# Finishing the last group of heads in one piece instead of two halves of queries

## The chip, the core and the metric

The kernel runs on one core of one Trainium2 chip. The core has a matrix engine (TensorE, PE in the profile, with its weight loads as PEld), a vector engine (VectorE, DVE), an activation engine (ScalarE, ACT), GpSimd (POOL) and SyncE (SP), which here issues most of the DMAs. Each engine works through its own instructions in the order in which they were written, and engines wait for each other by semaphores. The metric is the time of one execution on the device in microseconds (us).

## What is computed

One layer for 2048 tokens of width 640, with 32 heads of 20 dimensions. The tokens are normalised, and two branches are made from them. Branch A goes through four segments of 512 tokens one after another:

```python
logits = einsum(qs, ks) * scale + mask        # within the segment, causal
a_dot  = einsum(softmax(logits), vs)
a_mem  = (phi(qs) @ M) / (phi(qs) @ z + 1e-6) # memory of the segments before
o      = g * a_mem + (1.0 - g) * a_dot        # g: one gate per head
M, z   = M + phi(ks)^T @ vs, z + sum(phi(ks))
```

and its result is multiplied by `wo`. Branch B is a gated network on the same normalised tokens: `(sigmoid(x @ w_gate) * (x @ w_up)) @ w_down`, with 1536 hidden columns. The output is `x + A * silu(B)`.

## The kernel before

**The pieces of attention.** The 32 heads are treated as eight groups of four (`NG = 8`). A segment has four blocks of 128 queries and four blocks of 128 keys. A *unit* is one filling of a score tile `Sps` of 128 x 4 x 512 (four heads): `scores` writes it with TensorE (line 542), `exps` takes the exponential on ScalarE into `pt` (line 550) and cuts off the part above the diagonal with one GpSimd instruction for each key block in the unit (line 552). Two groups need five units, because a key block kb only meets the query blocks kb to 3: the last pair of groups (6 and 7 of segment 3) has the units (6: kb 0), (6: kb 1 and kb 3), (6: kb 2 and 7: kb 2), (7: kb 0) and (7: kb 1 and kb 3).

**The product with V.** In nearly all groups the product with V is made transposed (`attend_T`, tile `ApsT`). The last pair of groups takes another way, `attend` (lines 592 to 618): for each head and each query block from kb up, one small matmul (line 606, 128 x 21 out, the 21st column being the sum of the weights) adds into one PSUM tile `Aps` of 128 x 4 query blocks x 4 heads x 21. The parts of `Aps` written by the key block kb are the query blocks kb to 3. Key blocks come in the order in which the units deliver them; for group 7 this is 2, 0, 1, 3. So kb 1 is the third (12 matmuls) and kb 3 the fourth (4 matmuls, on query block 3 alone).

**Finishing a group.** `finalize(n, g, q0, q1)` divides by the sum of weights, applies the gate and adds to `odot`, which already holds the memory's part. It is four VectorE instructions over the query blocks q0 to q1:

```python
nc.vector.reciprocal(rd[:, 0:nq, :], Aps[:, q0:q1, :, DH])            # line 625
nc.vector.tensor_tensor(rd..., rd..., omg[...], op=ALU.mult)          # line 626
nc.vector.tensor_tensor(od..., Aps[:, q0:q1, :, 0:DH], rd..., mult)   # line 630
nc.vector.tensor_tensor(dst, dst, od, op=ALU.add)                     # line 632, dst: odot
```

Group 6 is finished by one such call over all four query blocks. Group 7 is finished by two: query blocks 0 and 1 after the third key block, query blocks 2 and 3 after the fourth.

**What stands around it.** All order is written out by hand: the program's text is a sequence of calls, and the events with times in `TIMES` and the dense work (the matmuls of branch B) are merged when the program is built, by a count of TensorE time (`fill`, `step`). `finalize` has no part in that count. In the last stage the dense work is the product with `w_down` (`do_down`, tile `yp`, 12 matmuls of 128 x 320 for each of 8 pieces; then ScalarE's tanh at line 448 into `t`, and VectorE's product at line 449 into `aa`). The PSUM tiles of all of this come from one pool of four buffers (`ps_d`).

**The tail** (lines 926 to 946). Two pieces of `yp` were held back. The first is made, then `tail_T4(0, 2)` transposes the last 128 columns of `odot` for the query blocks 0 and 1 on TensorE (line 517, tile `po`), ScalarE copies them to `oT` (line 518), and `tail_piece` multiplies by `wo` (line 526, tile `sp`, five matmuls of 128 x 320; the fourth of them takes its operand from `oTm`). `oTm` comes from `tail_sum` (line 512), one VectorE addition behind a transposing DMA of `odot` columns 384 to 511 (line 508), none of which are written by group 7's finishing. After the pieces of rows 0, the second held piece of `yp` and row block 1 comes `tail_T4(2, 4)` for the query blocks 2 and 3. The rest is products (line 528), additions (line 534) and output DMAs (lines 537 and 940).

Of the kernel before, what the change touches and what calls it, by code (L numbers as in the profile page):

```python
# [19 lines left out]
NG = 8  # L20
# [55 lines left out]
def kernel(  # L76
# [513 lines left out]
    acc = dict(group=None, todo=[])  # L590

    def attend(n, unit, pt):

        todo = acc["todo"] + [(p, pt) for p in unit]
        acc["todo"] = []
        for i, ((g, kb, c0, ncol, q0), t) in enumerate(todo):
            if acc["group"] is None:
                acc["group"], acc["blocks"], acc["fresh"] = g, 0, True
                acc["ps"] = ps_d.tile([P, 4, 4, E1], F32, name="Aps", tag="d")
            if acc["group"] != g or (acc["blocks"] == 0 and i > 0 and todo[i - 1][0][0] != g):  # L600
                acc["todo"] = todo[i:]
                break
            for r in range(4):
                for qb in range(kb, 4):
                    off = c0 + (qb - kb) * P
                    nc.tensor.matmul(acc["ps"][:, qb, r, :], lhsT=t[:, r, off:off + P],
                                     rhs=V[n % 2][:, kb, 4 * g + r, :],
                                     start=acc["fresh"], stop=True, skip_group_check=True)
                    acc["fresh"] = False
            acc["blocks"] += 1  # L610
            split = g == NG - 1
            if acc["blocks"] == 3 and split:
                finalize(n, g, 0, 2)
            if acc["blocks"] == 4:
                finalize(n, g, 2 if split else 0, 4)
                acc["group"] = None
                acc["todo"] = todo[i + 1:]
                break

    def finalize(n, g, q0, q1):  # L620

        s, Aps = seg[n], acc["ps"]
        nq = q1 - q0
        rd = opool.tile([P, 4, 4], F32, name="rd", bufs=3)
        nc.vector.reciprocal(rd[:, 0:nq, :], Aps[:, q0:q1, :, DH])
        nc.vector.tensor_tensor(rd[:, 0:nq, :], rd[:, 0:nq, :],
                                omg[:, 4 * g:4 * g + 4].unsqueeze(1).to_broadcast([P, nq, 4]), op=ALU.mult)
        dst = s["odot"][:, q0:q1, 4 * g * DH:(4 * g + 4) * DH]
        od = opool.tile([P, 4, 4 * DH], BF, name="od", tag="tb", bufs=1)[:, 0:nq, :]
        nc.vector.tensor_tensor(od.rearrange("p q (r e) -> p q r e", e=DH), Aps[:, q0:q1, :, 0:DH],  # L630
                                rd[:, 0:nq, :].unsqueeze(3).to_broadcast([P, nq, 4, DH]), op=ALU.mult)
        nc.vector.tensor_tensor(dst, dst, od, op=ALU.add)
# [134 lines left out]
    for p in range(0, OLD, 5):  # L767
        n, g = units[p][0], units[p][1][0][0]
# [16 lines left out]
    def old_attend(slot):  # L785
        attend(NSEG - 1, units[slot][1], pts[slot])
# [111 lines left out]
    for slot, (n, unit) in enumerate(units):  # L898
        if slot in visits:
            m, g, us = visits[slot]  # L900
# [73 lines left out]
```

## Time and profile before

| what | value |
|---|---|
| median of 3 runs | 321.15 us (320.79 to 321.5) |
| the profiled execution: time | 320.71 us |
| the profiled execution: span from first to last instruction | 319.0 us |
| granted TensorE clock, mean | 0.999 |
| PE busy | 311.4 us, 98% of the span |
| DVE, ACT, POOL busy | 229.8, 227.4, 135.4 us |
| DVE instructions | 505 |
| `attend`'s matmuls on `Aps` (line 606) | 80, from 290.1 to 304.3 us |

The page of the profile gives busy times and groups of instructions; the timeline gives each instruction with its start in us from the start of the span, its duration, its engine, its line, `out<-in`, its shape, how many were merged into the row, and in brackets how long the engine had been idle before it and which instruction's end released it. Matmuls overlap in the pipeline: their starts are recorded and their ends are modelled, so one row of merged matmuls runs from the first start to the last modelled end. The chain that ended last is followed back from the last instruction through whatever released each step.

### The profile page before, as it was taken

How to read it: one execution, taken by the hardware profiler on the slowest of the kernel's cores; microseconds unless marked ns; L12 is line 12 of the kernel's file. 1: busy time of each engine (PE TensorE's matmuls, PEld its weight loads, DVE VectorE, ACT ScalarE, POOL GpSimd, SP SyncE). 2: the span in 40 equal slices, each digit the busy share in tenths (PEclk: the TensorE clock that was granted, in tenths of full speed). 3: DMA queues.
4: the chain of work that ended last, by engine and by line, in shares of the span. 5: the costliest groups of instructions: out<-in, count | busy, mean ns of one | idle time of the engine just before them, and what ended most of it. 6: DMA issues, size and time to landing. Idle time of an engine off the chain costs nothing.

```text
span 319.0 us, 10076 instructions
## 1 busy us (share of the span) xinstructions
PE 311.4 (98%) x4244; PEld 167.2 (52%) x4244; DVE 229.8 (72%) x505; ACT 227.4 (71%) x228; POOL 135.4 (42%) x230
## 2 busy tenths in 40 slices
PE   7999999999999999999999999999999999999985
PEld 3644445664545445654675455545566545445653
DVE  6474356656769879997689999977787777635455
ACT  4623577787898877777998678788887766687611
POOL 1870036435263355235453445444443444535312
PEclk9999999999999999999999999999999999999999
DMA  7984986500751462406854534148433001250302
GB/s 253 369 328 134 311 212 173 130 20 4 218 164 56 144 109 105 105 23 199 212 171 123 143 93 126 47 150 202 148 90 116 11 23 43 106 125 2 101 17 82
DMA packets 56085, 41.36 MB, mean 130 GB/s; under 512 B 26952, under 2 KB 54664, under 8 KB 56040
## 3 DMA queue, kind: packets, MB, share of 16 engines
q1 hardware_dynamic: 53496, 35.97, 39.5%
q10 hardware_dynamic: 2544, 4.75, 4.0%
q8 instruction: 33, 0.54, 0.7%
q14 instruction: 12, 0.10, 0.1%
HBM read 19.90 MB, written 14.78 MB: 109 GB/s over the span
## 4 chain that ended last, share of the span: by engine, by line
PE 95%; DMA 2%; ACT 1%; DVE 1%; issue 0%; SPq 0%; ACTq 0%
PE up L124 11%; PE yp L124 11%; PE gp L124 10%; PE psq L124 10%; PE Sps L542 9%; PE gp L128 6%; PE up L128 6%; PE yp L128 6%; PE psv L124 5%; PE ApsT L566 5%; PE psq L128 4%; PE sp L124 3%; PE sp L128 3%; DMA Wv<-in_A_wv_dram 2%; PE sp L526 1%; PE psv L128 1%
## 5 line engine op out<-in xcount | busy, mean ns | idle before, releaser
L550 ACT ACTIVATE pt<-Sps 128x2048 bf16<-128x2048 f32 x80 | 150.2, 1878 | 40.2 <-PE Sps L542 35.4
L552 POOL TENSOR_SCALAR_AFFINE_SELECT pt<-pt 128x512 bf16<-128x512 bf16 x128 | 83.0, 665 | 156.8 <-ACT pt L550 156.7
L432 DVE SCALAR_TENSOR_TENSOR hT<-tg,up 128x512 bf16<-128x512 bf16 x48 | 32.4, 675 | 23.2 <-PE up L124 8.7
L124 PE MATMUL up<-xnT,Wu 128*128 128x512 bf16 x160 | 43.0, 380 | 0.0
L124 PE MATMUL yp<-Wd,hT 128*128 128x320 bf16 x257 | 39.9, 299 | 0.0
L124 PE MATMUL gp<-xnT,Wg 128*128 128x512 bf16 x150 | 39.3, 380 | 0.0
L421 ACT ACTIVATE tg<-gp 128x512 bf16<-128x512 f32 x48 | 28.6, 596 | 14.3 <-PE gp L124 10.9
L542 PE MATMUL Sps<-QT,KT 23*128 23x384 bf16 (+3 forms) x512 | 32.4, 300 | 0.2
L585 DVE STREAM_TRANSPOSE obT<-ob 128x512 bf16<-128x512 bf16 x30 | 21.1, 704 | 13.4 <-POOL ob L581 13.3
L124 PEld LDWEIGHTS <-hT 128*128 128x128 bf16 x257 | 23.5, 98 | 11.7 <-issue 3.2
L449 DVE SCALAR_TENSOR_TENSOR aa<-t,yp 128x320 bf16<-128x320 bf16 x32 | 15.3, 479 | 15.1 <-ACT t L448 14.9
L128 PE MATMUL gp<-xnT,Wg 128*32 128x512 bf16 x360 | 24.1, 380 | 0.0
L587 DVE STREAM_TRANSPOSE tb<-ApsT 128x512 f32<-128x512 f32 x30 | 21.2, 708 | 2.2 <-PE ApsT L566 2.1
L124 PEld LDWEIGHTS <-Wu 128*128 128x128 bf16 x160 | 14.3, 98 | 16.2 <-issue 3.2
L566 PE MATMUL ApsT<-pt,V 128*32 128x512 bf16 (+2 forms) x480 | 22.8, 299 | 0.0
L448 ACT ACTIVATE t<-yp 128x320 bf16<-128x320 f32 x32 | 14.0, 437 | 12.2 <-PE yp L124 10.3
L542 PEld LDWEIGHTS <-KT 23*128 23x128 bf16 x512 | 9.9, 92 | 24.3 <-issue 23.9
L124 PEld LDWEIGHTS <-Wg 128*128 128x128 bf16 x150 | 14.0, 98 | 16.0 <-issue 1.9
L128 PE MATMUL up<-xnT,Wu 128*32 128x512 bf16 x320 | 21.7, 380 | 0.0
L124 PE MATMUL psv<-Wv,xnT 128*128 128x320 bf16 x130 | 20.4, 299 | 0.3 <-ACT xnT L666 0.2
L581 POOL TENSOR_TENSOR ob<-tb,rb 128x320 bf16<-128x320 f32 x27 | 19.8, 733 | 2.3
L128 PE MATMUL yp<-Wd,hT 128*32 128x320 bf16 x508 | 20.0, 300 | 0.0
(122 smaller groups left out, 448.5 us busy)
## 6 DMA issues: line engine op xcount, KB each, us to landing
KT<-Kd SPq DMA_DIRECT2D x32, 80.0 KB
QT<-Qd SPq DMA_DIRECT2D x32, 80.0 KB
out_dram<-xt SPq DMA_DIRECT2D x14, 160.0 KB
Wg<-in_B_w_gate_dram ACTq DMA_DIRECT2D x1, 1920.0 KB
Wu<-in_B_w_up_dram ACTq DMA_DIRECT2D x1, 1920.0 KB
xt<-in_A_x_dram SPq DMA_DIRECT2D x3, 640.0 KB
Wd<-in_B_w_down_dram SPq DMA_DIRECT2D x1, 1920.0 KB
Xd<-xn SPq DMA_DIRECT2D x12, 160.0 KB
```

What stands on the lines that cost most here:

```text
L124: nc.tensor.matmul(out_, lhsT=lhsT, rhs=rhs, start=start, stop=stop, skip_group_check=True)
L128: nc.tensor.matmul(out_[cols], lhsT=lhsT[:, cols], rhs=rhs, start=start, stop=stop, tile_position=(0, 32 * r), skip_group_check=True)
L421: nc.scalar.activation(tg[:], gp[:], ACT.Tanh, scale=0.5)
L432: nc.vector.scalar_tensor_tensor(out=h[:], in0=seg[n]["tg"][:], scalar=1.0, in1=up[:], op0=ALU.add, op1=ALU.mult)
L449: nc.vector.scalar_tensor_tensor(out=s["aa"][j][:, hs], in0=t2[:], scalar=1.0, in1=yp[:], op0=ALU.add, op1=ALU.mult)
L542: nc.tensor.matmul(Sps[:, r, c0:c0 + ncol], lhsT=KT[32 * r:32 * r + DH + 3, g, kb * P:(kb + 1) * P], rhs=QT[32 * r:32 * r + DH + 3, g, q0: ...
L550: nc.scalar.activation(pt[:, :, 0:ntot], Sps[:, :, 0:ntot], ACT.Exp, scale=SCALE)
L552: nc.gpsimd.affine_select(out=pt[:, :, c0:c0 + P], in_=pt[:, :, c0:c0 + P], compare_op=ALU.is_ge, fill=0.0, base=0, pattern=[[0, 4], [1, P ...
L566: nc.tensor.matmul(ps[32 * r:32 * r + 32, q0:L], lhsT=Vflat[n % 2][:, off:off + 32], rhs=t[:, r, c0:c0 + ncol], start=(i == 0), stop=(i == ...
L581: nc.gpsimd.tensor_tensor(ob[:, :, 0:DH], tb[:, :, 0:DH], rb[:].unsqueeze(2).to_broadcast([P, L // 32, DH]), op=ALU.mult)
L585: nc.vector.transpose(s["obT", g // 4][:, g % 4, :], ob[:].rearrange("p b e -> p (b e)"))
L587: s["turn", g] = (lambda: nc.vector.transpose(tb[:].rearrange("p b e -> p (b e)"), ps[:]), quotients, turn_back)
```

## The change

Group 7 is no longer finished in two calls. The call over the query blocks 0 and 1 after its third key block goes, and the call after its fourth key block covers all four query blocks, as for group 6. No other call, tile or DMA is changed.

```diff
             acc["blocks"] += 1
-            split = g == NG - 1
-            if acc["blocks"] == 3 and split:
-                finalize(n, g, 0, 2)
             if acc["blocks"] == 4:
-                finalize(n, g, 2 if split else 0, 4)
+                finalize(n, g, 0, 4)
                 acc["group"] = None
                 acc["todo"] = todo[i + 1:]
                 break
```

## The prediction

> **What bounds the kernel now.** I read the page first, for what bounds the whole, then the timeline of the last 24 us, where group 7 is finished, then the waits and the chain there, and last a table of half microseconds around the spot.
>
> Page, busy times and the chain that ended last:
>
> ```profile
> PE 311.4 (98%) x4244; PEld 167.2 (52%) x4244; DVE 229.8 (72%) x505; ACT 227.4 (71%) x228; POOL 135.4 (42%) x230
> ...
> PE 95%; DMA 2%; ACT 1%; DVE 1%; issue 0%; SPq 0%; ACTq 0%
> ```
>
> TensorE bounds it: a microsecond in which TensorE stands still is one lost, unless it is waited for again later. DVE holds 1% of the chain, so there are places where the chain leaves TensorE. One is the edited place. Timeline of 295 to 319 us:
>
> ```profile
> 298.15 0.25 DVE L625 RECIPROCAL rd<-Aps 128x16 f32<-128x16 f32 x1
> ...
> 298.43 0.17 DVE L626 TENSOR_TENSOR rd<-rd,omg 128x16 f32<-128x16 f32 x1
> ...
> 298.64 0.49 DVE L630 TENSOR_TENSOR od<-Aps,rd 128x320 bf16<-128x320 f32 x1
> 299.17 0.32 DVE L632 TENSOR_TENSOR odot<-odot,od 128x320 bf16<-128x320 bf16 x1
> ...
> 299.38 0.75 PE L606 MATMUL Aps<-V,pt 128*128 128x21 bf16 x24
> ...
> 302.29 0.51 PEld L606 LDWEIGHTS <-pt 128*128 128x128 bf16 x13
> 302.43 0.45 PE L606 MATMUL Aps<-V,pt 128*128 128x21 bf16 x12
> ...
> 302.96 0.49 DVE L449 SCALAR_TENSOR_TENSOR aa<-t,yp 128x320 bf16<-128x320 bf16 x1 [0.56 <-ACT t L448]
> 303.37 0.20 DVE L625 RECIPROCAL rd<-Aps 128x8 f32<-128x8 f32 x1
> 303.61 0.17 DVE L626 TENSOR_TENSOR rd<-rd,omg 128x8 f32<-128x8 f32 x1
> 303.81 0.32 DVE L630 TENSOR_TENSOR od<-Aps,rd 128x160 bf16<-128x160 f32 x1
> 304.16 0.24 DVE L632 TENSOR_TENSOR odot<-odot,od 128x160 bf16<-128x160 bf16 x1
> 304.18 0.25 PE L606 MATMUL Aps<-V,pt 128*128 128x21 bf16 x4 [1.30 <-DVE od L630]
> ...
> 304.28 3.28 PE L124 MATMUL yp<-Wd,hT 128*128 128x320 bf16 x23
> 304.46 0.21 DVE L625 RECIPROCAL rd<-Aps 128x8 f32<-128x8 f32 x1
> ...
> 305.27 0.24 DVE L632 TENSOR_TENSOR odot<-odot,od 128x160 bf16<-128x160 bf16 x1
> ...
> 306.85 0.41 DVE L512 TENSOR_TENSOR oTm<-oTm,oT 96x512 bf16<-96x512 bf16 x1
> 307.27 0.23 PEld L517 LDWEIGHTS <-odot 128*128 128x128 bf16 x2
> ```
>
> The first four rows are group 6 finished in one piece. Then group 7: 12 matmuls of key block 1 at 302.43, and the 4 of key block 3 only at 304.18. They write query block 3, the first half's DVE work reads query blocks 0 and 1, and still they wait until its last read of `Aps` (line 630, to 304.13) is over: idle 1.30 us, released by DVE. The thirteenth weight load in the row at 302.29 is the first of key block 3's, so its `pt`, mask included, was there; only `Aps` was missing. The list of TensorE's waits in this stretch has this one entry alone, and the chain runs through it (ACT 302.49, DVE 302.96 to 304.14, PE 304.18).
>
> Half microseconds (busy of each engine with counts, clock, DMA share, GB/s):
>
> ```profile
> 303.00:303.50 0.50, 0.00 (x0) 0.00 (x0) 0.50 (x2) 0.00 (x0) 0.00 (x0) 1.00 0.92 210
> 303.50:304.00 0.50, 0.00 (x0) 0.00 (x0) 0.43 (x3) 0.00 (x0) 0.00 (x0) 1.00 0.17 33
> 304.00:304.50 0.50, 0.32 (x6) 0.28 (x6) 0.41 (x3) 0.00 (x0) 0.00 (x0) 1.00 0.00 0
> ```
>
> A whole microsecond has no matmul and only DVE at work; the DMA share is the transposing transfer into `oTm`, whose bytes end before 304.
>
> **The change part by part.** Sums are against the profiled execution: 319.0 us of span and 1.71 around it, 320.71, which is 0.44 below the median of the three runs.
>
> *Removed: the wait of key block 3.* Nothing on DVE now stands between the 12 matmuls and the 4. How long is the gap really? The idle column says 1.30, from the modelled end of the twelfth matmul (302.88) to 304.18. But small matmuls follow each other at their starts: the 24 of the row at 299.38 last 0.75 less 0.17 for the last one alone, so 0.58 for 23 steps, 0.025 a step. Listed one by one, the twelfth of key block 1 starts at 302.71; the next would start at 302.735 instead of 304.18: 1.44 us. The row of 24 is also followed by a `yp` matmul at 299.99, before its own end at 300.13. So I take 1.44, from recorded starts, and keep 1.30, the idle column, as the lower end. The Trainium skill (Perfetto Trace Analysis, section Tensor Engine Instruction) says that the profiler estimates the end of a matmul from its size instead of observing it; by that page the idle column understates this gain, and the trace agrees, with 299.99 against 300.13.
>
> *Removed: four DVE instructions.* Two halves cost 2 x (0.20 + 0.17 + 0.32 + 0.24) = 1.86 us busy; one piece costs as group 6's, 0.25 + 0.17 + 0.49 + 0.32 = 1.23. The 0.63 saved is worth nothing by itself: after 305.51 DVE idles 0.94 until its next product.
>
> *Moved: the finishing of query blocks 0 and 1 goes behind the 4 matmuls.* These then end at about 302.98 (302.735, three steps, 0.17). DVE is at line 449 until 303.45 anyway, so the first reciprocal stays at 303.37, and from there group 6's piece takes 299.49 - 298.15 = 1.34: all four blocks are in `odot` at 304.71, where before blocks 0 and 1 were at 304.40 and blocks 2 and 3 at 305.51. No DMA is issued by it, and it passes nothing on the queues of SP, POOL or ACT.
>
> *What is late next.* Everything behind on TensorE comes 1.44 earlier, and each item's supplier must follow:
> - The transposes of `odot` blocks 0 and 1 (weights at 307.27) move to 305.83; `odot` is ready at 304.71: cover 1.12, before 2.87. Without it, each further microsecond would be lost in full.
> - DVE's next product (306.44) moves to 305.00; the piece ends at 304.71: cover 0.29. It is queued behind it on DVE; were it late, it would delay the addition at line 512 first, which has the next cover.
> - Line 512 (306.85 to 307.26) moves to 305.41 to 305.82; its reader, the first matmul on `oTm`, has its weights at 307.79, then 306.35: cover 0.53, as now. Line 512 also needs the transposing DMA. Its bytes end before 304; when its semaphore came, the trace doesn't show, only that it was by 306.85. Bounds: it came with the bytes, 0 lost; or at 306.85, and then line 512 can't move, ends at 307.26, and the 306.35 load waits 0.91. The nearest row is the spill before it (line 504): bytes until shortly after 301, its successor released at 301.63. So some half microsecond, 304.5, and nothing is lost.
> - The PSUM buffer of `Aps` is free after line 630, at about 304.4 (before 305.23), for a tile that TensorE writes from 305.9 on: no wait.
> - ScalarE's copy of `po` keeps TensorE waiting 0.47 at 307.9, and the last DVE additions and stores take 3.7 us after the last matmul. Both hang on the matmuls alone and move with them.
>
> *Sum*: 319.0 - 1.44 = 317.56 of span; 319.27 for a profiled execution; 321.15 - 1.44 = 319.7 for the median, 0.45% less.
>
> **The rivals.**
> 1. *The transfer takes the place of the wait.* If the semaphore of the transposing DMA comes as late as 306.85, the load of `oTm` waits 0.91, and 0.53 of the gain stays: 320.6, 0.16% less. For it: the trace hides the landing. Against: bytes ended some 3 us before that.
> 2. *The change doesn't do what it says.* The 4 matmuls wait as long for something else, such as GpSimd's mask of key block 3 or the tile's former reader: 321.15. Against: the mask's row ends at 302.50 and the weights made from it were loaded before the stall.
> 3. *Slower: the piece, now whole, comes behind other DVE work.* Before, blocks 0 and 1 had 2.87 us until the transposes; now the transposes need the whole piece. If it ended after 305.83, TensorE would wait; from 307.27 the gain is gone, from 307.9 the kernel is slower by over 0.2%. The place would be behind the product at line 449 of the last `yp` before the transposes (308.07, then 306.63): from some 307.04 to 308.38, a wait of 2.55, 1.1 more than is won: 322.3. Against: the two calls stand in one event with nothing between them on DVE, and what stands ahead of the first half now (the product at 302.96) is what stands ahead of the piece then. For it: DVE is 72% busy, and in the rows above its instructions run one behind the other. The Trainium skill (Perfetto Trace Analysis, section Tensor Engine Instruction) states for DVE that its queue is strictly first in, first out, which speaks against joining the halves: a piece behind late work can't pass it. The trace agrees so far: the reciprocal of 303.37 started only as the product of 302.96 ended, though its matmuls had ended by 302.88.
>
> **How the numbers follow.** Forecast 0.83, rival 1 0.07, rival 2 0.05, rival 3 0.05. The three runs of before lie within 0.11% of their median, so a difference of about 0.2%, 0.64 us, is what can be told from none. Faster by more than that: the forecast, 0.83. Within it: rivals 1 and 2, 0.12. Slower: rival 3, 0.05. The forecast's own range is 321.15 less 1.44 or 1.30, with 0.4 of scatter on either side (the runs' half spread of 0.35 and a little for a second median): 319.3 to 320.25. The range goes a little lower, to 319.2, and up to rival 1 with a little scatter, 320.7.
>
> **What would show it.** Right: no wait of line 606 for DVE; 16 matmuls on `Aps` in one row from about 302.4, 0.55 long, and the 23 of `yp` from about 302.84; lines 625 to 632 twice each in the whole trace, all with 16 or 320 elements, and 501 DVE instructions; the piece from 303.4 to 304.7; line 512 near 305.4 and the weights of the transposes near 305.8 with no wait for DVE; a span near 317.6. Wrong: an idle time of TensorE before line 517 released by line 632 (rival 3), before the first matmul on `oTm` released by line 512 with DVE waiting for the DMA (rival 1), or a row of 4 matmuls on `Aps` still by itself (rival 2). The weakest term is the landing of the transfer; the stall itself is seen in one execution only, and a shorter one in the others would shrink the gain.

## The result and the profile after

The changed kernel takes 319.65 us (median of six runs, 319.48 to 320.62) against 321.49 us for the kernel before in the same comparison: ratio 0.9949, 95% interval 0.9932 to 0.9966. By the ratio that is 1.6 us less, between 1.1 and 2.2; the two medians are 1.84 apart. Forecast were 319.7 us and a gain of 1.44.

One number on the page misleads. The profiled execution of the changed kernel has a span of 318.9 us, as long as the 319.0 of before: it is the slowest of the six (320.62). Timeline of TensorE in the first 22 us, first the changed kernel, then the kernel before:

```profile
6.70 1.14 PE L124 MATMUL psv<-Wv,xnT 128*128 128x320 bf16 x5 [0.74 <-DMA Wv<-in_A_wv_dram]
...
11.54 2.88 PE L124 MATMUL psv<-Wv,xnT 128*128 128x320 bf16 x20
```

```profile
6.26 0.85 PE L124 MATMUL psv<-Wv,xnT 128*128 128x320 bf16 x5 [0.24 <-ACT xnT L666]
...
10.52 2.88 PE L124 MATMUL psv<-Wv,xnT 128*128 128x320 bf16 x20
```

The twenty matmuls start 1.02 us later in this execution, in which the first matmuls waited for the load of `Wv`. By the edited place the delay is 1.39 (303.82 against 302.43 for the first matmul of key block 1). Most of the last 0.37 arises at one row of `psv` at 168.5 us, of the same code in both: the delay is 1.12 ahead of it and 1.40 behind, and in the changed kernel TensorE stands idle there for 0.26 without a releaser that the profile shows. None of this lies near the edit. So the two profiles are compared from a mark inside them, the start of that first matmul of group 7's key block 1, to the start of the last addition on line 534. This *tail stretch* ends with these rows, first before, then changed:

```profile
315.99 0.32 DVE L534 TENSOR_TENSOR xt<-aa,xt 128x320 bf16<-128x320 bf16 x1
```

```profile
315.94 0.32 DVE L534 TENSOR_TENSOR xt<-aa,xt 128x320 bf16<-128x320 bf16 x1
```

It is 315.99 - 302.43 = 13.56 us before, and 315.94 - 303.82 = 12.12 us after: 1.44 less. The 13.56 come from one profile; for the other executions of the kernel before there are only the total times.

Timeline of the changed kernel at the edited place (its lines 622 to 629 are the lines 625 to 632 of before):

```profile
303.69 0.59 PEld L606 LDWEIGHTS <-pt 128*128 128x128 bf16 x16
303.82 0.55 PE L606 MATMUL Aps<-V,pt 128*128 128x21 bf16 x16
...
304.23 3.28 PE L124 MATMUL yp<-Wd,hT 128*128 128x320 bf16 x23
304.36 0.49 DVE L449 SCALAR_TENSOR_TENSOR aa<-t,yp 128x320 bf16<-128x320 bf16 x1 [0.56 <-ACT t L448]
304.76 0.25 DVE L622 RECIPROCAL rd<-Aps 128x16 f32<-128x16 f32 x1
305.04 0.18 DVE L623 TENSOR_TENSOR rd<-rd,omg 128x16 f32<-128x16 f32 x1
305.25 0.49 DVE L627 TENSOR_TENSOR od<-Aps,rd 128x320 bf16<-128x320 f32 x1
305.78 0.32 DVE L629 TENSOR_TENSOR odot<-odot,od 128x320 bf16<-128x320 bf16 x1
...
306.79 0.41 DVE L512 TENSOR_TENSOR oTm<-oTm,oT 96x512 bf16<-96x512 bf16 x1
307.21 0.23 PEld L517 LDWEIGHTS <-odot 128*128 128x128 bf16 x2
```

Both key blocks' 16 matmuls are one row with no wait, the 23 of `yp` begin 0.41 us behind its start (before: 304.28 - 302.43 = 1.85), and the piece on DVE ends at 306.10, 1.11 us ahead of the transposes' weights.

### The profile page after: what moved, and what is told of

It is laid out like the page before. It is cut to its first block, busy times and chain, and to the rows that moved or that the text cites. A ratio compares the mean times of both kernels' runs of the same rounds, so it can differ in the third digit from the quotient of the medians.

```text
span 318.9 us, 10072 instructions
## 1 busy us (share of the span) xinstructions
PE 311.6 (98%) x4244; PEld 166.9 (52%) x4244; DVE 229.3 (72%) x501; ACT 227.2 (71%) x228; POOL 135.1 (42%) x230
## 3 DMA queue, kind: packets, MB, share of 16 engines
q10 hardware_dynamic: 2544, 4.75, 4.0%
## 4 chain that ended last, share of the span: by engine, by line
PE 95%; DMA 2%; ACT 1%; DVE 1%; issue 0%; SPq 0%; ACTq 0%
PE up L124 11%; PE yp L124 11%; PE gp L124 10%; PE psq L124 10%; PE Sps L542 9%; PE gp L128 6%; PE up L128 6%; PE yp L128 6%; PE ApsT L566 5%; PE psv L124 5%; PE psq L128 4%; PE sp L124 3%; PE sp L128 3%; DMA xt<-in_A_x_dram 2%; PE sp L526 1%; PE psv L128 1%
```

## The experiments

All are read by the tail stretch, which comes from one profiled execution of each kernel; where a ratio is given, more executions were timed. Theory: the gain is TensorE's wait for the first half's reads of `Aps`, and nothing else.

**The changed kernel again, twice**, beside the other kernels.

> The changed kernel again, as the measure for the others. All expectations speak of the tail stretch: from the start of the first matmul of group 7's key block 1 on Aps to the start of the last addition on line 534 (before 315.99 - 302.43 = 13.56 us, changed kernel 315.94 - 303.82 = 12.12 us). Theory (the gain is TensorE's wait for the first half's reads of Aps, 1.44 us): 12.12 again, ratio about 0.9955. Rival (the opening of the kernel scatters and part of the measured gain is that): ratio nearer to 1, stretch unchanged.

Measured: ratio 0.9952 (0.9934 to 0.9969), stretch 315.05 - 302.93 = 12.12. So the gain is not one lucky comparison: ratio and stretch agree within the interval (1.44 of 321.2 is 0.9955). But this profile shows something that the first did not, at the transfer into `oTm` (SPq is the queue on which SyncE issues DMAs):

```profile
302.08 1.16 SPq L508 DMA_TRANSPOSE oTm<-Od  x1
...
306.57 0.57 PE L526 MATMUL sp<-Wo,oT 128*128 128x320 bf16 x3
...
306.69 0.42 DVE L512 TENSOR_TENSOR oTm<-oTm,oT 96x512 bf16<-96x512 bf16 x1 [0.71 <-DMA oTm<-Od]
...
307.17 0.10 PEld L526 LDWEIGHTS <-oTm 128*128 128x128 bf16 x1 [0.36 <-DVE oTm L512]
307.17 0.31 PE L526 MATMUL sp<-Wo,oTm 128*128 128x320 bf16 x1
...
307.41 0.72 PE L526 MATMUL sp<-Wo,oT 128*128 128x320 bf16 x4
```

Here the addition of line 512 waited for the transposing DMA, until 4.61 us after its issue, and the matmul on `oTm` waited for the addition. That is rival 1 at work, and yet the stretch is the same. The first changed profile shows why:

```profile
307.46 0.57 PE L526 MATMUL sp<-Wo,oT 128*128 128x320 bf16 x3
...
307.87 0.30 PE L526 MATMUL sp<-Wo,oTm 128*128 128x320 bf16 x1
...
308.30 0.72 PE L526 MATMUL sp<-Wo,oT 128*128 128x320 bf16 x4
```

The matmul behind the one on `oTm` starts 0.84 after the row of three in both (308.30 - 307.46 and 307.41 - 306.57), because it waits for ScalarE's copy of `po`. The one on `oTm` may come up to 0.3 later without loss; here it came 0.19 later.

> The changed kernel once more, beside the two above. Theory: stretch 12.12 whether line 512 waits for the DMA or not, since a wait of up to 0.31 there is taken up by the 0.47 us that the next matmul waits for ScalarE's copy; ratio about 0.9952.

Measured: ratio 0.9952 (0.9938 to 0.9966), stretch 315.85 - 303.73 = 12.12, and the wait for the DMA was there again (0.70 on DVE, 4.41 us after the issue).

**Both halves behind the fourth key block.**

```diff
-            if acc["blocks"] == 3 and split:
-                finalize(n, g, 0, 2)
             if acc["blocks"] == 4:
+                if split:
+                    finalize(n, g, 0, 2)
                 finalize(n, g, 2 if split else 0, 4)
```

> The two halves are kept, eight instructions on DVE, but both stand behind the fourth key block's matmuls. Theory (the wait alone): no wait of line 606 for DVE, the second half ends about 0.7 us later than the one piece, the next product and the addition of line 512 are late by some 0.4 us, which their covers hold: stretch 12.12, ratio about 0.9955. Rival (the gain is four DVE instructions fewer, 0.63 us of DVE, one piece instead of two): the gain goes, stretch near 13.5, ratio near 1.

```profile
303.06 0.55 PE L606 MATMUL Aps<-V,pt 128*128 128x21 bf16 x16
...
303.99 0.20 DVE L625 RECIPROCAL rd<-Aps 128x8 f32<-128x8 f32 x1
...
304.94 0.20 DVE L625 RECIPROCAL rd<-Aps 128x8 f32<-128x8 f32 x1
```

Measured: ratio 0.9948 (0.9930 to 0.9966), stretch 315.17 - 303.06 = 12.11. The eight DVE instructions are all there and the whole gain is too. One piece instead of two, and four instructions fewer, are worth nothing here; the place of the first half was everything.

**Two PSUM tiles for group 7, halves where they were.** The edit is shown in part; the rest of it makes `acc["ps"]` a list and keeps the mark of the first write for each tile.

```diff
+                acc["ps"] += [ps_d.tile([P, 4, 4, E1], F32, name="ApsB", tag="d") if g == NG - 1 else acc["ps"][0]]
...
-                    nc.tensor.matmul(acc["ps"][:, qb, r, :], lhsT=t[:, r, off:off + P],
+                    b = qb // 2 if g == NG - 1 else 0
+                    nc.tensor.matmul(acc["ps"][b][:, qb, r, :], lhsT=t[:, r, off:off + P],
...
-        s, Aps = seg[n], acc["ps"]
+        s, Aps = seg[n], acc["ps"][q0 // 2]
```

> The halves and their places are those of the kernel before, but group 7's query blocks 2 and 3 get a PSUM tile of their own. Theory (the wait is for the tile that both share, not for the split or its place): no wait of line 606 for DVE, stretch 12.1, ratio about 0.9955, unless the fifth tile in a pool of four makes some other matmul wait, which would be seen at its own row. Rival (a half finished between the key blocks holds TensorE whatever tile it reads): the 1.3 us idle before 4 matmuls stays, stretch 13.56, ratio 1.

Measured: ratio 0.9950 (0.9932 to 0.9968), stretch 314.78 - 302.67 = 12.11. Timeline:

```profile
302.92 0.30 PE L608 MATMUL ApsB<-V,pt 128*128 128x21 bf16 x6
...
303.44 0.20 DVE L627 RECIPROCAL rd<-Aps 128x8 f32<-128x8 f32 x1
...
304.40 0.20 DVE L627 RECIPROCAL rd<-ApsB 128x8 f32<-128x8 f32 x1
```

Key block 3's four matmuls run straight on (the last six of the row on `ApsB`), although the first half is called ahead of them: TensorE had waited for the tile that the half reads, not for the half. The Trainium skill (PSUM — Partial Sum Buffer, section PSUM bank collisions raise a hardware error) tells kernels to guard PSUM by bank and group of 32 partitions, not by address; the two traces agree, with 1.30 us of idle for other columns of one tile and none for another tile. The kernel's text names no semaphore: the wait that the trace shows was put in when the program was built. Whether it goes by the tile or by the bank that the tile lies in, and what the hardware would do without it, no run here separates.

**The wait made shorter and longer.** First, the first half copies its part of `Aps` into SBUF and works there:

```diff
+        if nq == 2 and q0 == 0:
+            ac = opool.tile([P, 2, 4, E1], F32, name="ac", bufs=1)
+            nc.vector.tensor_copy(ac[:], Aps[:, q0:q1])
+            Aps = ac
```

> The kernel before, but the first half first copies its part of Aps (128 x 168) into SBUF by one DVE instruction and works from there. Theory (TensorE waits for the last read of Aps, no longer): the copy takes about 0.3 us as the read of 128 x 160 did, so the last read ends near 303.7 instead of 304.13 in the time of before, the wait is about 0.43 shorter, stretch 13.56 - 0.43 = 13.1. Rival (TensorE waits until the half is finished in odot): the half is 0.3 longer, stretch 13.9.

Second, its product on line 630 is done four times, with the same result each time:

```diff
-        nc.vector.tensor_tensor(od.rearrange("p q (r e) -> p q r e", e=DH), Aps[:, q0:q1, :, 0:DH],
-                                rd[:, 0:nq, :].unsqueeze(3).to_broadcast([P, nq, 4, DH]), op=ALU.mult)
+        for _ in range(4 if nq == 2 and q0 == 0 else 1):
+            nc.vector.tensor_tensor(od.rearrange("p q (r e) -> p q r e", e=DH), Aps[:, q0:q1, :, 0:DH],
+                                    rd[:, 0:nq, :].unsqueeze(3).to_broadcast([P, nq, 4, DH]), op=ALU.mult)
```

> The kernel before, with the first half's product on line 630, the last read of Aps, done four times instead of once: 3 x 0.35 = 1.05 us more between the key blocks. Theory: the wait grows by all of it, idle 2.35, stretch 13.56 + 1.05 = 14.6. Rival (some of the wait is set by something other than DVE's reads): less than that is added.

Timeline of the first, then of the second:

```profile
304.00 0.33 DVE L626 COPY ac<-Aps 128x168 f32<-128x168 f32 x1
...
304.38 0.25 PE L606 MATMUL Aps<-V,pt 128*128 128x21 bf16 x4 [0.86 <-DVE ac L626]
```

```profile
304.42 1.40 DVE L631 TENSOR_TENSOR od<-Aps,rd 128x160 bf16<-128x160 f32 x4
...
305.87 0.25 PE L606 MATMUL Aps<-V,pt 128*128 128x21 bf16 x4 [2.38 <-DVE od L631]
```

Measured: stretch 316.19 - 303.06 = 13.13 (expected 13.1) and 317.68 - 303.04 = 14.64 (expected 14.6). The wait goes with the last read of `Aps` to within 0.05 us, in both directions, and all of it arrives at the end of the tail stretch (-0.43 and +1.08 against 13.56).

**The piece made longer.** The same loop around the product, in the changed kernel and for the whole of group 7, three times in the first kernel and five times in the second:

```diff
+        for _ in range(3 if g == NG - 1 else 1):
```

> The changed kernel, with group 7's product on line 627 done three times instead of once: the piece is 2 x 0.53 = 1.06 us longer. By the covers as the prediction had them (0.29 until the next product, then 0.53 until the first matmul on oTm: 0.82 in a row) 0.24 is lost: stretch 12.36. If the wait of 0.47 for ScalarE's copy, which comes right behind that matmul, takes up what line 512 is late, only the transposes' cover of 1.11 counts: stretch 12.12.

> The changed kernel, with group 7's product on line 627 done five times: the piece is 4 x 0.53 = 2.12 us longer. Theory (behind the cover of 1.11 of the transposes every further microsecond is lost in full): 1.0 lost, stretch 13.1; by the prediction's covers in a row (0.82) 1.3 lost, stretch 13.4. Rival (DVE is not near the path): 12.12.

Measured: 314.94 - 302.83 = 12.11, nothing lost by 1.05 us more on DVE (the second of its two expectations, 12.12), and 315.69 - 302.74 = 12.95, 0.83 lost. Timeline of the second:

```profile
306.80 0.32 DVE L630 TENSOR_TENSOR odot<-odot,od 128x320 bf16<-128x320 bf16 x1
...
307.18 0.11 PEld L517 LDWEIGHTS <-odot 128*128 128x128 bf16 x2 [1.08 <-DVE odot L630]
307.18 0.28 PE L517 MATMUL po<-ident,odot 128*128 128x128 bf16 x2 [0.75 <-DVE odot L630]
```

The transposes start 4.44 us into the stretch instead of 3.53 (307.35 - 303.82 in the changed kernel): 0.91 late. A little is won back behind them, since ScalarE's copy of `po` no longer stands behind the tanh of the held piece (it starts 0.32 after the transposes instead of 0.53). So 0.83 was lost where 1.0 was expected, and the cover of the changed kernel is a little over 1 us.

**Line 512 ahead of the piece**, to see when the transfer lands and what a late piece costs:

```diff
-    at(SLOTS - 0.001, 0, tail_sum)
+    at(SLOTS - 0.645, 0, tail_sum)
```

> The changed kernel, with the addition of line 512 put ahead of the piece on DVE, so that the landing of the transposing DMA is seen as DVE's idle time, and so that a late piece shows rival 3 in its price. By the prediction's estimate (landing some half microsecond behind the bytes, 2.9 us after the DMA's issue) line 512 starts at 304.5 in the time of before, the piece ends near 306.2, TensorE waits 0.4 at the transposes, stretch 12.5. By the waits seen in the repeat of the changed kernel and in the kernel with the hidden copies (line 512 released by the DMA 4.6 and 4.4 us after its issue; elsewhere 4.0 or less) it starts between 305.4 and 306.2, the piece ends between 307.1 and 307.9, TensorE waits 1.3 to 2.1: stretch 13.4 to 14.2, as slow as the kernel before or slower.

Timeline, and then in stretches of 1 us the busy time of PE, PEld, DVE, ACT and POOL with counts, the granted clock, the DMA share and GB/s:

```profile
302.15 1.16 SPq L508 DMA_TRANSPOSE oTm<-Od  x1
...
306.90 0.42 DVE L512 TENSOR_TENSOR oTm<-oTm,oT 96x512 bf16<-96x512 bf16 x1 [2.93 <-DMA oTm<-Od]
...
308.65 0.29 PE L517 MATMUL po<-ident,odot 128*128 128x128 bf16 x2 [2.00 <-DVE odot L629]
...
310.97 2.70 PE L124 MATMUL yp<-Wd,hT 128*128 128x320 bf16 x12
```

```profile
308.00:309.00 1.00, 0.35 (x4) 0.32 (x5) 0.96 (x4) 0.03 (x1) 0.00 (x0) 1.00 0.00 0
309.00:310.00 1.00, 1.00 (x7) 0.48 (x6) 0.50 (x2) 0.34 (x1) 0.00 (x0) 0.69 0.00 0
310.00:311.00 1.00, 1.00 (x6) 0.54 (x5) 0.37 (x1) 0.00 (x0) 0.00 (x0) 0.50 0.00 0
311.00:312.00 1.00, 1.00 (x5) 0.58 (x4) 0.49 (x1) 0.00 (x0) 0.21 (x1) 0.50 0.00 0
312.00:313.00 1.00, 1.00 (x6) 0.59 (x5) 0.00 (x0) 0.00 (x0) 1.00 (x1) 0.60 0.00 0
```

Measured: the transfer releases line 512 4.75 us after its issue; the transposes start 5.70 into the stretch, 2.17 late; and the stretch is 318.69 - 302.95 = 15.74, worse than either expectation (3.62 lost). The other 1.45 go with the clock: it was granted at 0.50 from about 309.4 to 312.8 (by the means of 0.69 and 0.60 in the two stretches at the edges), while twelve matmuls of `yp` took 2.70 instead of the 1.79 of before. From the row of four `sp` matmuls at 309.40 to the next piece at 313.50 it is 4.10 us, in the changed kernel 310.76 - 308.30 = 2.46; of these 1.64 more, 0.20 were won at ScalarE's copy ahead of them. A piece of DVE work queued behind a late transfer makes this kernel slower than before, as rival 3 had it in kind.

**The copies of ScalarE covered.** In the changed kernel the whole `odot` is ready at once, so its transposes can move up:

```diff
-    finish(held[1][3])
+    for _ in range(6):
+        next(held[1][3])
     tail_T4(0, 2)
+    finish(held[1][3])
...
+    tail_T4(2, 4)
     tail_piece(1, 1)
     tail_add(1, 0, 1, nc.vector)
-    tail_T4(2, 4)
```

> The changed kernel, with the transposes of odot blocks 0 and 1 put into the middle of the held piece of yp (behind six of its twelve matmuls), and those of blocks 2 and 3 ahead of the second product of row block 1 instead of behind it. The copies of ScalarE that TensorE waited for, 0.47 and 0.25 us, then have matmuls beside them. Theory (after the change the whole odot is ready early enough, at 304.7 in the time of before, so they can move up): stretch 12.12 - 0.72 = 11.40, ratio about 0.9933. Rival (another wait takes their place, such as the addition of line 512 for oTm, or PSUM buffers): stretch near 12.1, ratio near 0.9955.

Measured: ratio 0.9930 (0.9913 to 0.9948), 319.08 us, stretch 314.49 - 302.72 = 11.77, so 0.35 won and not 0.72. The first suspicion was line 512's wait, since here too it was released by the DMA late (4.39 us after the issue). The next kernel takes that away by giving both products of row block 0 their four other parts first:

```diff
-    tail_piece(0, 0)
-    tail_piece(0, 1)
+    tail_row0()
...
+        for cs in ((0, 1, 2, 4), (3,)):
+            for half in range(2):
+                hs = slice(half * HD, (half + 1) * HD)
+                for c in cs:
+                    nc.tensor.matmul(sps[half][:], lhsT=s["oTm" if c == 3 else "oT"][:, c, 0:P], rhs=Wo[:, c, hs],
+                                     start=(c == 0), stop=(c == 3), skip_group_check=True)
```

> The kernel with the hidden copies, and both products of row block 0 first take their four other parts each and then, in two last matmuls, the part from oTm that waits for the DMA. Theory (0.36 of the 0.72 us expected there went into line 512's wait for the DMA): the reader of line 512 comes about 0.7 us later, the wait goes, stretch 12.12 - 0.72 = 11.40, ratio about 0.9930. Rival (the late products of row block 0 delay DVE, or a PSUM buffer): stretch 11.77 or more.

```profile
306.13 1.25 PE L537 MATMUL sp<-Wo,oT 128*128 128x320 bf16 x8
306.20 0.42 DVE L512 TENSOR_TENSOR oTm<-oTm,oT 96x512 bf16<-96x512 bf16 x1 [0.65 <-DMA oTm<-Od]
...
307.22 0.43 PE L537 MATMUL sp<-Wo,oTm 128*128 128x320 bf16 x2
...
307.49 1.79 PE L124 MATMUL yp<-Wd,hT 128*128 128x320 bf16 x12
```

Measured: ratio 0.9936 (0.9921 to 0.9951), 318.93 us, stretch 314.20 - 302.50 = 11.70. There is no gap left in this row block (ten matmuls in 307.49 - 306.13 = 1.36 us), and still only 0.42 is won: both the theory of the 0.36 and the expected 0.72 were wrong. The 0.72 were idle times of the weight loads (0.47 and 0.25). By the starts of the matmuls in the changed kernel, at a step of 0.136, the gaps are 308.30 - 307.87 - 0.136 = 0.29 and 312.86 - 312.64 - 0.136 = 0.08 us: 0.38 in all, which is about what the two kernels won. Both beat the changed kernel on their own group's medians (319.08 against 319.61, 318.93 against 319.73) and by the stretch; the intervals of the ratios overlap with its.

## Why the prediction was right, point by point

- *The wait of key block 3 goes, worth 1.44.* Right: 13.56 to 12.12 in three profiles of the changed kernel, and the two kernels with a shorter and a longer wait move it by -0.43 and +1.08. That the median of 319.65 lies within 0.05 of the forecast is partly luck: the kernel before stood at 321.49 in this comparison instead of 321.15, and the medians differ by 1.84. Taking the gap from the starts (1.44) instead of the idle column (1.30) was right; the same care was missing later for the 0.47.
- *Four DVE instructions fewer are worth nothing.* Right: with all eight behind the fourth key block the stretch is 12.11.
- *The piece from 303.37 to 304.71.* Right: 306.10 - 303.82 = 2.28 into the stretch, forecast 304.71 - 302.43 = 2.28. The cover of the transposes, forecast 1.12, is 1.11 in the profile, and the kernels with a longer piece put it between 1.05 and 2.1, with 0.91 late transposes for 2.1 more.
- *Line 512: the transfer's landing estimated at 304.5, 2.9 us after the issue, so nothing lost.* This step failed in its reason, not in its sum, and that the sum held was luck: the room that took up the late landing was not counted in the prediction (next point). In five profiles in which DVE waited for it the release came 4.4 to 4.75 us after the issue (4.61 and 4.41 in the changed kernel, 4.39, 4.49 and 4.75 in others), 2.2 to 2.7 after the last bytes, where the spill before it, taken as the nearest row, had half a microsecond. In the first profile of the changed kernel it was at most 3.82, in the kernels with the halves behind and with two tiles at most 4.00 and 4.05 (306.29 - 302.29 and 305.75 - 301.70, line 512 without a wait). So the landing scatters. And the changed kernel does wait on DVE for the DMA in two of three profiles: rival 1's mechanism was there. The Trainium skill (DMA: Bandwidth & Descriptors, section Anatomy of one DMA — SWDGE (gpsimd) path) gives about 2 us of fixed cost for a DMA issued through GpSimd, most of it between the last byte and the semaphore; this transfer was issued by SyncE, its five late releases lie a little above that figure, and the one of at most 3.82 below it (at most 1.6 behind the bytes). As a bound it would have been nearer than half a microsecond.
- *The cover of line 512 of 0.53 and, for rival 1, 0.91 lost.* Mis-sized: some 0.3 more is free behind it, since the next matmul waits for ScalarE's copy anyway. That is why the late landing cost nothing.
- *Rival 2* (the wait stays) fell with the first row of the new timeline. *Rival 3* did not happen, but its place is real: with line 512 ahead of the piece, late DVE work took the transposes 2.17 us back.

## What to carry to other kernels

A tile that one engine is still adding to should not be read in parts by another in between: in this kernel the next write waited for the read even on other columns, and early finishing then cost the reader's whole chain up to its last read. Finish it whole if the consumer has cover, or give the early part its own tile; here both won the same 1.44 us. And size a stall of TensorE by the starts of its matmuls, and compare two executions from a mark close to the edit: the spans of these two profiles differ by 0.1 us, the stretch by 1.44.

## What the runs showed of the hardware that was not expected

- The semaphore of the transposing DMA came 2.2 to 2.7 us behind its last bytes in five profiles, and at most 1.6 behind in another, with the same bytes. Counted from the issue it was 4.39 to 4.75 us in the five and at most 3.82, 4.00 and 4.05 in three others.
- The clock fell to 0.50 after TensorE's 2.00 us of idle in one kernel, and not after 2.38 us in another (1.00 throughout), so the length of a gap alone does not decide it. The Trainium skill (TensorE: Matmul & The Clock Gate, section Part 1: The HAM clock gate) ties the gate to free-running windows of about 3.4 us and has it fall after an idle one. The time at half clock here, about 3.4 us, agrees; the gap of 2.00 us ahead of it is shorter than a window, and there the measurement decides. One run each: that the gap is what brought the clock down is inferred from their order in time.
